# Attention with row maxima: the last step of each unit's maximum made on POOL instead of DVE, with new planner constants

## The chip, the cores and the metric

The kernel runs on one core of one Trainium2 chip. The metric is the device time of one execution in microseconds (us). Five engines work at once, each through its own instruction queue: PE (TensorE, matrix products), ACT (ScalarE, activations), DVE (VectorE, reductions and element-wise work), POOL (GpSimd, element-wise work on SBUF only) and SP, which here issues all transfers. PEld stands for PE's loads of stationary operands.

## The reference, cut to what matters

Two layers share their weights. Each is an attention block and a gated feed-forward block, both behind a layer norm and added to the residual stream. There are 2048 tokens of width 512 in 32 heads of 16, and the hidden width is 1792.

```python
qkv = layernorm(x) @ wqkv                   # q, k, v: 32 heads of 16
scores = einsum("bhqd,bhkd->bhqk", q, k) * 16 ** -0.5
p = softmax(scores, axis=-1)
x = x + reshape(einsum("bhqk,bhkd->bhqd", p, v)) @ wo
h = layernorm(x)
x = x + (gelu(h @ w_gate) * (h @ w_up)) @ w_down
# the same block of two a second time
```

The softmax subtracts each query's maximum over all 2048 keys. The change touches how that maximum is put together.

## The kernel before, in words

**Units.** The work of attention is cut into 72 units. A unit is a group of four heads and a block of queries: 512 queries in seven of the nine query blocks, 256 in the last two of the second layer. Four heads lie in four row groups of PE, 32 partitions each, of which 16 hold the head's coordinates.

**First pass (`p1_emit`, L1579 and L1594).** For 128 queries (`qt`), one head (`j`) and one block of 512 keys (`kb`), PE makes a score tile of 128 x 512 in PSUM, and DVE reduces it, or two tiles at once, to one maximum per query. The maxima go to `PM[:, slot, (qt, kb, j)]`. So a unit of 512 queries gives 4 x 4 x 4 = 64 numbers per partition, a unit of 256 queries 32.

**Folds (`f_emit`, L1398, L1405, L1408; `kd`, L1210; fused step L1589).** For some of these tiles the maximum of two key blocks is taken at once. POOL makes the difference of the two key blocks in `KD`, PE multiplies the queries by it, ACT takes the positive part into a slot of `PT` (a part of `SCR`), and a fused DVE step adds the other block's scores and reduces. The skipped block's entry in `PM` is set to -3e38 by POOL. A fold moves work from DVE to ACT. The planner decides how many there are.

**End of a unit's first pass (`fin`, L950 and L952).** One DVE `tensor_reduce` takes the maximum over the four key blocks, negates it and writes it to `MSEL` in bf16. A DVE transpose puts it into `MT`. Then SP writes it by four small transfers (`negmax`, L971) into an extra row of the queries' operand `QT`. The keys' operand `KT` holds a constant in the same row, +1, which comes from `KBIAS`. So the second pass's product gives score minus maximum with no further step. The three units whose first pass is split (`fin_part`, `fin_rest`, `merge`) and the half unit at the end go other ways with the same signs.

**Second pass (`p2_tile`, `p2_emit`, L1449 and L1425; `pv_emit`, L1473; `nrm`).** PE makes the scores again, with keys as rows, ACT takes the exponential into `PT`, and PE multiplies by the values, with a column of ones that sums the weights, into PSUM bank 7. At a unit's end ACT copies that sum to `ACCS` (L1017), and POOL makes the reciprocals (L1027, a power of -1) and multiplies (L1032).

**The rest.** Projections, the output product and the feed-forward products go through L670, 256-wide where the query block is 256. `evac` and its like (L687, L685) copy their results out of PSUM on ACT or DVE, by how far the first pass is ahead of the second. Some element-wise work follows on POOL: the gate product L1173, the residual sum L1047, parts of the layer norm L719 to L727. In the narrow blocks DVE can do the gate product itself (L1165). L1618 is a filler product of zeros, put where PE would idle.

**The order.** No hardware decides it. `_build` holds a planner, which keeps one clock per engine from stated durations, and in each round takes the next work for PE: a first-pass tile, a second-pass tile, both, a weighted-sum step, a piece of a projection, or a filler. From that come all queues, and `_Sched` puts in the semaphores. Element-wise steps are generators (`_Chain`) that go on when the planner's clocks say that their inputs are ready. Nineteen constants steer the choices. `PLAN` gives a new set for each stretch of 16 first-pass pairs, 129 sets in all. Among them are `SPC`, `SPLIT`, `S1C`, `S2C` (when both passes' tiles are sent together), `LAG` and `LAGT` (how far the first pass may lead), `FL`, `GL`, `FX` (when to fold), and `PIECE`, `GP` (how many matmuls of a projection go in one piece).

Of the kernel before, what the change touches and what calls it, by code (L numbers as in the profile page):

```python
# [6 lines left out]
BF = mybir.dt.bfloat16  # L7
# [303 lines left out]
def _build(nc, x_in, wqkv, wo, wg, wu, wd, out, layer_blocks=((512, 512, 512, 512), (512, 512, 512, 256, 256)),  # L311
# [16 lines left out]
    with es:  # L328
        def sb(name, shape, dt):
            return es.enter_context(nc.sbuf_tensor(name, shape, dt))  # L330
# [1521 lines left out]
```

## Time and profile before

| what | value |
|---|---|
| runs | 2537.78, 2538.1, 2541.32 us (median 2538.1) |
| profiled execution: own time, span | 2542.32 us, 2540.6 us |
| granted clock of PE | 0.998 |
| busy: PE, DVE, ACT, POOL | 2434.9, 2421.7, 2371.5, 591.8 us |
| first-pass reduces on DVE (L1594) | x2489, 2204.7 us |
| exponentials on ACT (L1425) | x2521, 2017.5 us |
| fillers on PE (L1618) | x2408, 425.9 us |
| end-of-unit reduces on DVE (L950) | x69, 17.5 us |
| folds (L1589) | x185 |

The profile is that of one execution, and its own time stands beside the runs' median. Busy time is the time in which an engine had an instruction at work. Matmuls overlap each other, so a PE that is busy is not a PE at its peak. In the rows of groups, the count and busy time come first, then the mean length of one in nanoseconds, then the idle time of the engine just before them with what ended it.

### The profile page before, as it was taken

What the parts mean: (1) busy time and instruction counts of PE and PEld (TensorE: products, weight loads), DVE (VectorE), ACT (ScalarE), POOL (GpSimd) and SP (SyncE); (2) the same over time, 40 slices, a digit from 0 to 9 for tenths busy, and PEclk for the clock granted to TensorE, in tenths of its full rate; (3) what the DMA queues carried; (4) which work ended last, traced back from release to release, by engine and by line L of the source; (5) the groups of instructions that cost most, each with busy time, mean ns of one, the idle gap of its engine ahead of it and who ended that gap; (6) DMA issues with size and microseconds to landing.
All of it is one profiled execution on the core that took longest, in us unless ns stands there. A gap on an engine that the chain in (4) does not pass through costs nothing.

```text
span 2540.6 us, 67774 instructions
## 1 busy us (share of the span) xinstructions
PE 2434.9 (96%) x29660; PEld 1170.1 (46%) x29864; DVE 2421.7 (95%) x3192; ACT 2371.5 (93%) x3270; POOL 591.8 (23%) x743
## 2 busy tenths in 40 slices
PE   8999999999999999999999999999999999999999
PEld 3444443454434444344434455434544445544546
DVE  7999999999999999999998999999999999999993
ACT  7899998999999999999978999999999999989995
POOL 4011122312332213321123211241113211332300
PEclk9999999999999999999999999999999999999999
DMA  3110000000000000000000000000000000000000
GB/s 100 39 56 6 4 9 1 4 2 2 8 1 4 2 3 8 2 4 17 10 6 1 17 2 2 8 3 11 2 8 2 6 6 3 4 3 13 3 8 5
DMA packets 27416, 25.05 MB, mean 10 GB/s; under 512 B 9456, under 2 KB 26096, under 8 KB 27120
## 3 DMA queue, kind: packets, MB, share of 16 engines
q1 hardware_dynamic: 27120, 20.71, 2.8%
q8 instruction: 234, 3.83, 0.6%
q14 instruction: 62, 0.51, 0.1%
HBM read 9.70 MB, written 2.10 MB: 5 GB/s over the span
## 4 chain that ended last, share of the span: by engine, by line
PE 43%; ACT 29%; DVE 26%; issue 1%; POOL 0%; ACTq 0%
ACT SCR L1425 27%; DVE PM L1594 25%; PE PS L1579 13%; PE PS L670 11%; PE PS L1473 9%; PE PS L1449 4%; PE PS L1618 4%; ACT SCR L1405 1%; PE PS L1398 1%; PE PS L768 0%; DVE SCR L1589 0%; ACT AO L1045 0%; ACT XNT L687 0%; ACT ATTT L687 0%; ACT ACCS L1017 0%
## 5 line engine op out<-in xcount | busy, mean ns | idle before, releaser
L1594 DVE TENSOR_REDUCE PM<-PS 128x1 f32<-128x512 f32 (+1 forms) x2489 | 2204.7, 949 | 51.9 <-PE PS L1449 23.3
L1425 ACT ACTIVATE SCR<-PS 128x1024 bf16<-128x1024 f32 (+1 forms) x2521 | 2017.5, 896 | 57.8 <-PE PS L1449 39.5
L1579 PE MATMUL PS<-KT,QT 32*128 32x512 bf16 x3911 | 1006.4, 384 | 36.2 <-DVE PM L1594 19.4
L1449 PE MATMUL PS<-QT,KT 32*128 32x512 bf16 (+1 forms) x4608 | 940.0, 360 | 11.5 <-ACT SCR L1425 8.5
L1473 PE MATMUL PS<-VP,SCR 128*128 128x51 bf16 (+1 forms) x16384 | 806.8, 187 | 12.4 <-ACT SCR L1425 9.5
L1473 PEld LDWEIGHTS PS<-VP,SCR 128*128 128x128 bf16 x16384 | 571.7, 96 | 498.9 <-issue 439.1
L1579 PEld LDWEIGHTS PS<-KT,QT 32*128 32x128 bf16 x3911 | 240.3, 91 | 506.9 <-DVE PM L1594 286.6
L1618 PE MATMUL PS<-WV,ZER 128*128 128x240 bf16 x2408 | 425.9, 267 | 7.7 <-ACT SCR L1425 6.9
L1027 POOL TENSOR_TENSOR RL<-ACCS,CM 128x16 f32<-128x16 f32 (+1 forms) x63 | 173.4, 2753 | 1008.7 <-ACT ACCS L1017 1008.4
L1449 PEld LDWEIGHTS PS<-QT,KT 32*128 32x128 bf16 x4608 | 232.7, 91 | 89.8 <-ACT SCR L1425 60.5
L1618 PEld LDWEIGHTS PS<-WV,ZER 128*128 128x128 bf16 x2408 | 184.6, 97 | 73.7 <-issue 53.0
L1173 POOL TENSOR_TENSOR HT<-HT,AO 128x512 bf16<-128x512 bf16 (+1 forms) x112 | 123.1, 1101 | 261.9 <-ACT AO L1171 261.8
L1210 POOL TENSOR_TENSOR KD<-KT 128x512 bf16<-128x512 bf16 x71 | 81.8, 1154 | 207.3 <-PE PS L1398 188.2
L1405 ACT ACTIVATE SCR<-PS 128x512 bf16<-128x512 f32 (+1 forms) x132 | 103.7, 786 | 23.5 <-PE PS L1398 23.2
L1589 DVE CUSTOM_DVE_ANT_0 SCR<-PS,SCR 128x512 bf16<-128x512 f32 x185 | 119.6, 686 | 4.0 <-PE PS L1579 2.7
L670 PE MATMUL PS<-XNT,WU 128*128 128x512 bf16 (+1 forms) x444 | 116.4, 354 | 6.6 <-issue 5.5
L670 PE MATMUL PS<-WD,HT 128*128 128x512 bf16 x378 | 114.3, 380 | 8.0 <-issue 6.5
L670 PE MATMUL PS<-XNT,WG 128*128 128x512 bf16 (+1 forms) x488 | 117.1, 357 | 2.1 <-issue 1.0
L1047 POOL TENSOR_TENSOR X<-X,AO 128x512 f32<-128x512 f32 x45 | 57.1, 1268 | 212.1 <-ACT AO L1045 212.0
L1152 ACT ACTIVATE HT<-PS 128x512 bf16<-128x512 f32 (+1 forms) x126 | 69.1, 550 | 31.8 <-PE PS L670 29.3
L1171 ACT ACTIVATE AO<-PS 128x512 f32<-128x512 f32 (+1 forms) x112 | 65.6, 586 | 2.0 <-PE PS L670 1.3
L670 PEld LDWEIGHTS PS<-XNT,WG 128*128 128x128 bf16 x504 | 39.6, 97 | 54.8 <-issue 31.1
(106 smaller groups left out, 883.2 us busy)
## 6 DMA issues: line engine op xcount, KB each, us to landing
KT<-SG SPq DMA_DIRECT2D x64, 64.0 KB
QT<-MT SPq DMA_DIRECT2D x236, 1.0 KB
QT<-SG SPq DMA_DIRECT2D x56, 64.0 KB
out_dram<-AO SPq DMA_DIRECT2D x16, 128.0 KB, 1.7
WG<-in_B_w_gate_dram SPq DMA_DIRECT2D x4, 448.0 KB, 5.0
WU<-in_B_w_up_dram SPq DMA_DIRECT2D x4, 448.0 KB, 4.8
WD<-in_B_w_down_dram SPq DMA_DIRECT2D x4, 384.0 KB, 4.9
QT<-MT SPq DMA_DIRECT2D x68, 0.5 KB
```

The lines of the kernel that those rows point to most:

```text
L670: ins = e.matmul(out_ap, lhsT=l, rhs=r_, start=(i == 0), stop=(i == n - 1))
L1027: emit("pool", lambda e: e.tensor_tensor(RL[:, s, 0:4 * nq], lsum, CM1[:, 0:4 * nq], op=ALU.pow), r=[("ACCS", s), ("CM1",)], w=[("RL", s)] ...
L1173: emit("pool", lambda e, ft=ft, o=o: e.tensor_tensor(HT[:, ft, 0:n], HT[:, ft, 0:n], AO[:, o, 0:n], op=ALU.mult), r=[("AO", o), ("HT", ft) ...
L1210: emit("pool", lambda e: e.tensor_tensor(KD[:, s, :], KT[:, g, ka * 512:(ka + 1) * 512], KT[:, g, kb * 512:(kb + 1) * 512], op=ALU.subtrac ...
L1405: emit("act", lambda e: e.activation(PT[:, s0:s0 + cnt, :], PS[:, bk:bk + cnt, :], ACTF.Relu), r=bks, w=[("PT", s0 + d) for d in range(cnt ...
L1425: emit("act", lambda e: e.activation(dst, src, ACTF.Exp, scale=DH ** -0.5), r=[BK[bk + i] for i in range(cnt)], w=[("PT", i) for i in slot ...
L1449: ins = e.matmul(bank(bk)[:, i * n:(i + 1) * n], lhsT=KT[32 * j:32 * j + 32, g, kt * 128:(kt + 1) * 128], rhs=QT[32 * j:32 * j + 32, s, 0: ...
L1473: ins = e.matmul(acc, lhsT=PT[:, slot, i * n + qt * 128:i * n + (qt + 1) * 128], rhs=AP(VP, (kt * H + 4 * g + j) * 17, [[NTT * H * 17, 128 ...
L1579: ins = e.matmul(bank(b), lhsT=QT[32 * j:32 * j + 32, s, qt * 128:(qt + 1) * 128], rhs=KT[32 * j:32 * j + 32, g, kb * 512:(kb + 1) * 512], ...
L1589: emit("dve", lambda e, i=i, b=b, sl=sl: e.tensor_tensor_reduce(PT[:, sl, :], bank(b), PT[:, sl, :], 1.0, -3.0e38, ALU.add, ALU.max, po[:, ...
L1594: emit("dve", lambda e: e.tensor_reduce(po, PS[:, bs[0]:bs[0] + cnt, :], axis=AX.X, op=ALU.max), r=bks, w=[("PM", sm) + h[1:] for h in hs] ...
L1618: return e.matmul(PS[:, b, NACC:512], lhsT=ZER[:, :], rhs=WV[:, 0, 0:512 - NACC], start=(b != 7), stop=(b != 7), skip_group_check=True)
```

## The change

The end-of-unit maximum of 65 of the 72 units is made by POOL. `fin` hands those units to the new `fin_pool`, which makes the maximum of two numbers as x - y, its positive part, plus y. It does that for key blocks 0 with 1 and 2 with 3 in one go, then for the two results: six POOL instructions. The transpose stays on DVE and now waits for POOL. The last four units and the three split ones stay on the DVE reduce. The maximum is no longer negated, so the constant in the keys' extra row becomes -1, and `fin_part`, `fin_rest` and `merge` change their signs to match.

`PLAN` gets two more columns, `PB` and `OVF`. `PB` over 1 holds a weighted-sum step back until `PB` of them are ready while PE is in row groups (33 sets). `OVF` lets projection work run over while PE works as one array (49 sets are not 0). The other columns change in 126 of 129 sets. New code for a layer norm on POOL (`ln_pool`) is switched off (`LNP=0`), and `NSG=3` keeps the number of staging buffers. A few of the sets and all of the rest:

```diff
 PLAN = [
-    (0.0, 0.25, 0.45, 0.42, 0.3, -0.05, 1, 1, 70, 84, 8, 60, 0.3, 2.0, 0, 2, 2, 2, 7),
-    (0.1, 0.2, 0.65, 0.62, 0.3, -0.05, 1, 1, 62, 84, 8, 60, 0.3, 2.0, 0, 2, 2, 2, 7),
...
+    (0.1, 0.1, 0.45, 0.42, 0.3, -0.05, 1, 1, 62, 84, 8, 60, 0.3, 2.0, 0, 2, 2, 1, 7, 1, 0.0),
+    (0.1, 0.1, 0.45, 0.42, 0.3, -0.05, 2, 1, 62, 84, 8, 60, 0.1, 2.0, 0, 2, 2, 2, 7, 1, -0.1),
...
-            emit("pool", ... e.affine_select(KBIAS[:, 0:1], KBIAS[:, 0:1], [[0, 1]], ALU.not_equal, 1.0,
+            emit("pool", ... e.affine_select(KBIAS[:, 0:1], KBIAS[:, 0:1], [[0, 1]], ALU.not_equal, -1.0,
...
 def fin_part(u):
-            emit("dve", lambda e: e.tensor_reduce(mo, pin, axis=AX.X, op=ALU.max, negate=True),
+            emit("dve", lambda e: e.tensor_reduce(mo, pin, axis=AX.X, op=ALU.max),
...
 def fin_rest(u):
-            emit("dve", lambda e: e.tensor_scalar(do, pin, -1.0, 0.0, op0=ALU.mult, op1=ALU.min),
+            emit("dve", lambda e: e.tensor_scalar(do, pin, 0.0, None, op0=ALU.max),
...
+        def fin_pool(u):
+            s1 = u % n_ahead
+            nq = units[u][3] // 128
+            pv = PM[:, s1, 0:nq * 4 * NKB].rearrange("p (a k j) -> p a k j", a=nq, j=4)
+            mo = MSEL[:, s1, 0:4 * nq].rearrange("p (j a) -> p a j", j=4)
+            kk = [("PM", s1, qt, kb, j) for qt in range(nq) for kb in range(4) for j in range(4)]
+            yield ("pool", kk, [])
+            for w, x, y, o, ok, d in ((2, pv[:, :, 0::2, :], pv[:, :, 1::2, :], pv[:, :, 1::2, :], kk, 0.055 * nq / 4),
+                                      (1, pv[:, :, 1, :], pv[:, :, 3, :], mo, [("MSEL", s1)], 0.03 * nq / 4)):
+                emit("pool", lambda e, x=x, y=y: e.tensor_tensor(x, x, y, op=ALU.subtract), r=kk, w=kk, dur=0.19 + d)
+                emit("pool", lambda e, x=x: e.tensor_scalar(x, x, 0.0, None, op0=ALU.max), r=kk, w=kk, dur=0.19 + d / 2)
+                emit("pool", lambda e, x=x, y=y, o=o: e.tensor_tensor(o, x, y, op=ALU.add), r=kk, w=ok, dur=0.19 + d)
+            yield ("dve", [("MSEL", s1)], [("MT", s1)])
+            emit("dve", lambda e: e.transpose(MT[:, s1, :], MSEL[:, s1, :]),
+                 r=[("MSEL", s1)], w=[("MT", s1)], dur=0.13)
+            fin_rec.add(u)
+            add(negmax(u), -1e6 + u)
...
 def fin(u):
-            emit("dve", lambda e: e.tensor_reduce(mo, pin, axis=AX.X, op=ALU.max, negate=True),
+            if FNP and u < NU - 4 and u not in split and NKB == 4:
+                return add(fin_pool(u), -1e6 + u)
+            emit("dve", lambda e: e.tensor_reduce(mo, pin, axis=AX.X, op=ALU.max),
...
+            if PB > 1 and mode[0] == "row" and G is not None and G < now + 0.4 and work and work[-1][0] == 1:
+                n_rdy = 0
+                for q in pvq[:PB]:
+                    if est([("PT", q[1])]) <= now + 0.03:
+                        n_rdy += 1
+                if n_rdy < PB and pt_busy.count(None) > 1:
+                    work.pop()
             for pr, t, cost, fn, due, at in work:
                 over = (SO if seam else OV if can_p2[0] else URG) if due < pos["p1"] - DUEM and pr > 1 else 0.0
+                if mode[0] == "full" and pr > 1:
+                    over += OVF
```

More of the change, by code (lines that the diff above doesn't have):

```diff
@@ L311, in _build @@
 def _build(nc, x_in, wqkv, wo, wg, wu, wd, out, layer_blocks=((512, 512, 512, 512), (512, 512, 512, 256, 256)),
-           n_ahead=6, n_pre=6, S1C=0.45, S2C=0.42, OV=0.3, PD=80, FDUE=20, LIM=-0.05, NT=1, AHD=2.0, DUEM=2, FDL2=0, OPD=12, URG=0.3, ft_tok=512, n_pt=8, n_qt=8, SPLIT=0.15, SPC=0.1, PVC=47, WARM=0.55, WARML=0.42, NPV=7, BOOST=0.0, LAG=62, LAGT=84, GP=2, SING=0, DUE=0, END=360, LAGE=10, FD=205, FDL=-10, QD=32, KD_=16, VD=20, FL=8, FMAX=6, NKD=2, FLOOK=2, FX=0.3, GF=1, NSPL=3, HSPL=0, TSPL=1, HNA=3, TNA=3, HV=16, TW=0.95, HF=60, VS=14, SO=1.0, SF=1, SP=0, FAST=1, TG=0, GS=2, P2B=1, PIECE=2, GL=60, GLE=20, HARD=-1e9):
+           n_ahead=6, n_pre=6, S1C=0.45, S2C=0.42, OV=0.3, PD=80, FDUE=20, LIM=-0.05, NT=1, AHD=2.0, DUEM=2, FDL2=0, OPD=12, URG=0.3, ft_tok=512, n_pt=8, n_qt=8, SPLIT=0.15, SPC=0.1, PVC=47, WARM=0.55, WARML=0.42, NPV=7, BOOST=0.0, LAG=62, LAGT=84, GP=2, SING=0, DUE=0, END=360, LAGE=10, FD=205, FDL=-10, QD=32, KD_=16, VD=20, FL=8, FMAX=6, NKD=2, FLOOK=2, FX=0.3, GF=1, NSPL=3, HSPL=0, TSPL=1, HNA=3, TNA=3, PB=1, OVF=0.0, LNP=0, FNP=1, NSG=3, LNT=12, HV=16, TW=0.95, HF=60, VS=14, SO=1.0, SF=1, SP=0, FAST=1, TG=0, GS=2, P2B=1, PIECE=2, GL=60, GLE=20, HARD=-1e9):
     S = x_in.shape[1]
@@ L350, in _build @@
         QT = sb("QT", [128, n_qt, 512], BF)
-        SG = sb("SG", [128, 3, 512], BF)
+        SG = sb("SG", [128, NSG, 512], BF)
         HT = sb("HT", [128, NFT, ft_tok], BF)
@@ L368, in _build @@
         DW = sb("DW", [128, NSB, 16], F32)
+        LS = sb("LS", [128, 512], F32) if LNP else None
         KD = sb("KD", [128, NKD, 512], BF)
@@ L535, in _build @@
         for j in range(4):
-            emit("pool", lambda e, j=j: e.affine_select(KBIAS[:, 0:1], KBIAS[:, 0:1], [[0, 1]], ALU.not_equal, 1.0,
+            emit("pool", lambda e, j=j: e.affine_select(KBIAS[:, 0:1], KBIAS[:, 0:1], [[0, 1]], ALU.not_equal, -1.0,
                                                         base=-(32 * j + 1), channel_multiplier=1),
@@ L708, in ln_fast, with ln_sum @@
                 at["xn"] = i
+        def ln_sum(i, xa, xk, first, col, dur):
+            yield ("pool", [xk] + ([] if col == 0 else [("LNS", i)]), [("LS",)])
+            first()
+            w = D // 4
+            while w >= 16:
+                yield ("pool", [], [])
+                emit("pool", lambda e, w=w: e.tensor_tensor(LS[:, 0:w], LS[:, 0:w], LS[:, w:2 * w], op=ALU.add),
+                     r=[("LS",)], w=[("LS",)], dur=0.18 + w / 520.0)
+                w //= 2
+            yield ("dve", [("LS",)], [("MV", i)])
+            emit("dve", lambda e, i=i: e.tensor_reduce(MV[:, i, col:col + 1], LS[:, 0:16], axis=AX.X, op=ALU.add),
+                 r=[("LS",)], w=[("MV", i)], dur=0.09)
@@ new lines, in ln_pool, with first, second @@
+        def ln_pool(tts, x_of, ready, at):
+            for i, tt in enumerate(tts):
+                xa, xk = x_of(tt)
+                yield ("cond", lambda tt=tt: ready(tt))
+                def first():
+                    emit("pool", lambda e: e.tensor_tensor(LS[:, 0:D // 2], xa[:, 0:D // 2], xa[:, D // 2:D], op=ALU.add),
+                         r=[xk], w=[("LS",)], dur=0.18 + D / 1040.0)
+                def second():
+                    emit("pool", lambda e: e.tensor_scalar(LS[:, 0:D], xa, 1.0, LNS[:, 2, i:i + 1], op0=ALU.mult, op1=ALU.add),
+                         r=[xk, ("LNS", i)], w=[("LS",)], dur=0.77)
+                    emit("pool", lambda e: e.tensor_tensor(LS[:, 0:D], LS[:, 0:D], LS[:, 0:D], op=ALU.mult),
+                         r=[("LS",)], w=[("LS",)], dur=0.18 + D / 520.0)
+                    emit("pool", lambda e: e.tensor_tensor(LS[:, 0:D // 2], LS[:, 0:D // 2], LS[:, D // 2:D], op=ALU.add),
+                         r=[("LS",)], w=[("LS",)], dur=0.18 + D / 1040.0)
+                yield from ln_sum(i, xa, xk, first, 0, 0)
+                yield ("pool", [("MV", i)], [("LNS", i)])
+                emit("pool", lambda e, i=i: e.tensor_scalar(LNS[:, 2, i:i + 1], MV[:, i, 0:1], -1.0 / D, None, op0=ALU.mult),
+                     r=[("MV", i)], w=[("LNS", i)], dur=0.24)
+                yield from ln_sum(i, xa, xk, second, 1, 0)
+                yield ("pool", [("MV", i)], [("LNS", i)])
+                emit("pool", lambda e, i=i: e.tensor_scalar(LNS[:, 0, i:i + 1], MV[:, i, 1:2], 1.0 / D, LN_EPS, op0=ALU.mult, op1=ALU.add),
+                     r=[("MV", i), ("LNS", i)], w=[("LNS", i)], dur=0.24)
+                emit("pool", lambda e, i=i: e.tensor_tensor(LNS[:, 1, i:i + 1], LNS[:, 0, i:i + 1], CM05[:, i:i + 1], op=ALU.pow),
+                     r=[("LNS", i), ("CM05",)], w=[("LNS", i)], dur=0.59)
+                yield ("cond", lambda i=i: at["tr"] > i - 2)
+                yield ("pool", [xk, ("LNS", i)], [("XN", i % 2)])
+                emit("pool", lambda e, i=i, xa=xa: e.tensor_scalar(
+                    XN[:, i % 2, :], xa, LNS[:, 2, i:i + 1], LNS[:, 1, i:i + 1], op0=ALU.add, op1=ALU.mult),
+                    r=[xk, ("LNS", i)], w=[("XN", i % 2)], dur=0.77)
+                at["xn"] = i
@@ L784, in ln_to_xnt @@
             else:
-                add((ln_fast if fast else ln_head)(tts, x_of, ready, at), due)
+                by_pool = LNP and tag != ("in", 0) and not fast and (tag == ("mid", NL - 1) or tts[0] < LNT)
+                add((ln_fast if fast else ln_pool if by_pool else ln_head)(tts, x_of, ready, at), due)
             for i, tt in enumerate(tts):
@@ L795, in ln_to_xnt @@
             locks["XN"] = False
-        sg_free = [0, 1, 2]
+        sg_free = list(range(NSG))
         def proj(W, wkey, c, cols, n, tts):
@@ L917, in merge @@
             yield ("pool", [("MSEL", s1), ("MSB", i)], [("DW", i)])
-            emit("pool", lambda e: e.tensor_tensor(DW[:, i, 0:4 * nq], sgn[0], sgn[1], op=ALU.subtract),
+            emit("pool", lambda e: e.tensor_tensor(DW[:, i, 0:4 * nq], sgn[1], sgn[0], op=ALU.subtract),
                  r=[("MSB", i), ("MSEL", s1)], w=[("DW", i)], dur=0.2)
@@ L1634, in _build @@
                 if stretch[0] < len(PLAN):
-                    SPC, SPLIT, S1C, S2C, OV, LIM, NT, P2B, LAG, LAGT, FL, GL, FX, AHD, DUE, DUEM, PIECE, GP, NPV = PLAN[stretch[0]]
+                    SPC, SPLIT, S1C, S2C, OV, LIM, NT, P2B, LAG, LAGT, FL, GL, FX, AHD, DUE, DUEM, PIECE, GP, NPV, PB, OVF = PLAN[stretch[0]]
                 stretch[0] += 1
```

254 rows, old and new, of the table PLAN are left out of this document.

## The prediction

> **What bounds the kernel now.** I read the head of the page and its chain that ended last (shares by engine), then the busy times by stretch (columns: PE, PEld, DVE, ACT, POOL).
>
> ```profile
> span 2540.6 us, 67774 instructions
> PE 2434.9 (96%) x29660; PEld 1170.1 (46%) x29864; DVE 2421.7 (95%) x3192; ACT 2371.5 (93%) x3270; POOL 591.8 (23%) x743
> ...
> PE 43%; ACT 29%; DVE 26%; issue 1%; POOL 0%; ACTq 0%
> ...
> 100.00:1200.00 1100.00, 1057.26 (x13058) 503.35 (x13143) 1081.74 (x1457) 1058.84 (x1376) 259.11 (x331) 1.00 0.03 9
> 1200.00:1500.00 300.00, 288.60 (x3240) 131.09 (x3265) 281.94 (x361) 271.25 (x384) 76.25 (x94) 1.00 0.03 7
> 1500.00:2440.00 940.00, 908.25 (x11562) 440.46 (x11642) 920.11 (x1168) 896.42 (x1288) 224.87 (x248) 1.00 0.02 5
> 2440.00:2540.60 100.60, 95.25 (x1218) 58.48 (x1216) 57.16 (x91) 72.54 (x103) 3.32 (x8) 0.95 0.02 6
> ```
>
> Between 100 and 2440 us DVE idles 18.3 + 18.1 + 19.9 = 56 us, ACT 41 + 29 + 44 = 114 us. So DVE is the tighter of two nearly full engines: what leaves DVE shortens the span as long as ACT can follow, and ACT has some 58 us more room. PE's 96% is softer: it holds 2408 filler matmuls (L1618), issued only where nothing else was ready. POOL is three quarters idle. The chain passes between the three full engines in thousands of short pieces, so none of them is the bound alone. Next, the groups with the shapes kept apart.
>
> ```profile
> L1594 DVE TENSOR_REDUCE PM<-PS 128x2 f32<-128x1024 f32 x1237 | 1491.9, 1219 | 37.9 <-PE PS L1449 17.3 <-PE PS L1579 9.0 <-PE PS L1398 0.2
> L1594 DVE TENSOR_REDUCE PM<-PS 128x1 f32<-128x512 f32 x1252 | 844.3, 683 | 13.9 <-PE PS L1449 6.0 <-PE PS L1579 2.0 <-PE PS L1398 0.7
> L952 DVE STREAM_TRANSPOSE MT<-MSEL 128x32 bf16<-128x32 bf16 x69 | 14.6, 212 | 2.4
> L950 DVE TENSOR_REDUCE MSEL<-PM 128x16 bf16<-128x64 f32 x53 | 14.2, 268 | 1.8
> ```
>
> The score reduces are nearly all of DVE. The step that the change moves is the last row: once per unit, it reduces the four key blocks' maxima to one. Its place, in the timeline of DVE (start, length):
>
> ```profile
> 74.16 1.22 DVE L1594 TENSOR_REDUCE PM<-PS 128x2 f32<-128x1024 f32 x1
> 75.41 0.27 DVE L950 TENSOR_REDUCE MSEL<-PM 128x16 bf16<-128x64 f32 x1
> 75.71 0.21 DVE L952 STREAM_TRANSPOSE MT<-MSEL 128x32 bf16<-128x32 bf16 x1
> 75.85 0.65 DVE L1589 CUSTOM_DVE_ANT_0 SCR<-PS,SCR 128x512 bf16<-128x512 f32 x1
> 76.42 0.08 DVE L1589 DVE_READ_ACCUMULATOR2_ANT PM<- 128x1 f32 x1
> ```
>
> **The sum.** Counts are from the instruction orders of the two built kernels, durations from this execution (span 2540.6, own time 2542.3; the median shown is 2538.1, 4.2 lower).
>
> *Reduce removed from DVE.* 65 of the 69 go (53 wide, 12 narrow; the last four units and the three split ones keep theirs). From its start to the transpose's is 75.71 - 75.41 = 0.30 us. The narrow form means (17.5 - 14.2) / 16 = 0.206 us, say 0.24 with its gap. 53 x 0.30 + 12 x 0.24 = 18.8 us off DVE, 16.7 by busy time alone. The 65 transposes stay.
>
> *Fewer folds.* A fold lets ACT take the positive part of a difference of two blocks, so that DVE skips one of them and runs a fused step on the other. The new constants make 173 instead of 185. Plain heads: 3726 cost 2204.7 us merged, 0.592 each; 24 more are +14.2 us. Fused steps follow each other at 0.61 us (76.42 to 77.03 and on; the first of that row at 0.57), 12 fewer are -7.3. DVE: +6.9 us. ACT loses 12 x 103.7 / 185 = 6.7 us.
>
> *Exponentials and evacuations.* 12 double exponentials become 24 single: at 1.068 and 0.610 us that is +1.8 us on ACT. Five 256-wide gate products return from ACT with POOL (0.449 us each, -2.2) to DVE (0.425, +2.1); two 0.69-us evacuations leave DVE and a 256-wide one (0.4) comes: -1.0; ACT gets +0.8. DVE in all: -18.8 + 6.9 + 2.1 - 1.0 = -10.8 us; ACT: -6.7 + 1.8 - 2.2 + 0.8 = -6.3 us. Both fall, so ACT does not become the limit in DVE's place.
>
> *PE's switches.* PE works in row groups (L1579, L1449, L1398) or as one array (the others). The order changes between the two 5518 times before, 5342 after: 176 fewer, where the constants PB (hold a weighted-sum step until several are ready) and OVF (let projections run over) act. Price:
>
> ```profile
> 700.82 0.39 PE L670 MATMUL PS<-XNT,WG 128*128 128x512 bf16 x1
> 701.14 0.39 PE L1579 MATMUL PS<-KT,QT 32*128 32x512 bf16 x2
> 701.46 0.82 PE L670 MATMUL PS<-XNT,WG 128*128 128x512 bf16 x3
> ```
>
> Three array matmuls in a row take 0.82, so they follow at (0.82 - 0.39) / 2 = 0.215 us; after a single one the row group starts 0.32 later. A switch costs 0.105 us, 176 of them 18.5 us of PE. Where PE idles or fills it buys nothing (0). PE has 43% of the chain that ended last: 8 us at most. I take 4, since DVE's waits for L1449 and L1579 come to only 34 us.
>
> *Tail.* After the last score matmul 40 exponential tiles of 512 remain instead of 38: +1 us of ACT with DVE idle.
>
> *POOL's chain and the new wait.* Each unit gets six POOL steps: subtract, positive part and add over 32 elements, then over 16. The nearest rows: tensor-tensor on 16 elements (L918) 0.220 us, on 272 (L926) 0.658, so 1.7 ns per element; tensor-scalar on 1 element (L723) 0.243, on 512 (L727) 0.774, so 1.0 ns. That makes 0.247 + 0.275 + 0.247 + 0.22 + 0.26 + 0.22 = 1.47 us. Dependent POOL steps start 0.08 to 0.10 after each other's end:
>
> ```profile
> 7.55 0.24 POOL L719 TENSOR_SCALAR LNS<-MV 128x1 f32<-128x1 f32 x1 [2.38 <-DVE MV L717]
> 7.87 0.57 POOL L721 TENSOR_TENSOR LNS<-LNS,CM 128x1 f32<-128x1 f32 x1
> 8.53 0.25 POOL L723 TENSOR_SCALAR LNS<-MV 128x1 f32<-128x1 f32 x1
> ```
>
> Five such gaps make 1.9 us. The upper bound is the strided 128x256 row (L1032), 0.621 us a step: 4.2 us. I take 1.9, the small rows being the near ones. POOL's busy time rises by about 65 x 1.47 = 95 us, to 27%. The transpose now waits on DVE for that chain, and the next score reduces queue behind it, and PE's score banks behind them. In the new order 2.4 to 7.7 us of other DVE work stand between a unit's last reduce and its transpose (62 units counted, median 3.8), so a chain of 1.9 us costs 0. The query maxima reach PE some 4 us later; score heads lead exponential tiles by 58 or more from head 200 to 3700 (46 before), about 34 us of reduces, so that hides too. KBIAS's sign and the other sign changes cost nothing: same instructions.
>
> The Trainium skill (GPSIMD Engine Reference, Engine selection) speaks against the change: elementwise work on VectorE, about 2x slower on GpSimd. By that rule, with the chain on the path, each unit would pay 1.9 for 0.3 us, +104 us in all; the trace, with POOL idle for 77% of the span, speaks for cover instead.
>
> Sum: -10.8 - 4 + 1 = -13.8 us. The profiled execution would take 2528.5, the median 2524.3 us.
>
> **Rivals.**
>
> *DVE stalls at the transpose (slower).* POOL's work stands in one queue. Ahead of the chain are 23 times a key difference (1.15 us), 12 times a gate product that waits for an ACT copy, 11 times the normalisation of 0.4 to 0.6 us behind a power of 1.6 to 2.9 us that waits for ACT. For: POOL's waits for ACT are its longest (1008 us before L1027). Against: the order gives most units over 3.4 us. Against the counted covers a chain of 3.5 us stalls 18 units by 11 us in sum; with 13.8 us gained the break-even is about 3.6 us. At 4.2 us, 42 units lose 34 us: 2538 - 14 + 34 = 2558. Smaller excesses end between 2533 and 2543.
>
> *The gain is swallowed (same).* Nearly every constant row is changed (126 of 129), and none of that idle time can be priced from here. If DVE's 56 us of mid-span idle grow by a quarter, 14 us, the time stays at 2538. For: ACT is at 96%, so a bad mix of the two in one stretch costs at once. Against: both engines have less to do.
>
> *The constants gain more (faster still).* If the same 56 us fall by a quarter, and the switches bring their full 8 us: 2524 - 14 - 4 = 2506.
>
> That the reduce stays on DVE is excluded: only 7 of these are left in the new DVE order.
>
> SBUF contention is the other way a busier POOL could hurt DVE. The Trainium skill (GPSIMD Engine Reference, Specifications) has it only for DVE work in a two-port mode or with two SBUF inputs. The reduces on L1594 read PSUM, and I give it no chance of its own.
>
> **The numbers.** Forecast, between 2513 and 2533: 0.60. More gain: 0.16. Swallowed, 2533 to 2543: 0.13. Stalls or a worse mix, over 2543: 0.11. A measurement tells about 0.2% (5 us) here. So faster 0.76, same 0.13, slower 0.11. The range goes from the bigger gain's end, 2507, to 2541, where the swallowed case is mostly inside; some 2 in 10 stay outside.
>
> **What would show it.** Right: DVE busy near 2411 and ACT near 2365, POOL near 690; POOL steps at 0.2 to 0.28 us; the transposes with no idle before them named after POOL; some 5340 switches and a chain with less PE. Wrong: idle before the transpose released by POOL, of tenths of a us in dozens of units (first rival), or L1594's idle above 52 us, waiting for L1449 and L1579 (second).

## The result and the profile after

| kernel | median (us) | range (us) |
|---|---|---|
| before, runs beside after | 2539.71 | 2537.78 to 2541.44 (4) |
| before, in the three later sessions | 2537.61, 2537.94, 2537.31 | 2535.4 to 2541.4 (19, 19, 12) |
| after | 2524.30 | 2523.95 to 2524.91 (4) |

After takes 0.994 of before (95% interval 0.9923 to 0.9957). The forecast was 2524.3. Two of the four runs of before beside after took 2541 us, as did later runs with a clock of 0.998, while the rest had 1.0. Against the medians of the later sessions the gain is 13.0 to 13.6 us, and that is the figure used below. The profiled execution of before had 12.4 us of half clock near its end, so the two spans differ by 18.4 us, some 5 more than the medians.

The page of after: head, busy times, shares of the chain that ended last, then the busy times by stretch (PE, PEld, DVE, ACT, POOL).

```profile
span 2522.2 us, 68091 instructions
PE 2409.2 (96%) x29682; PEld 1161.1 (46%) x29881; DVE 2403.7 (95%) x3131; ACT 2353.2 (93%) x3267; POOL 683.9 (27%) x1119
PE 42%; DVE 32%; ACT 24%; issue 1%; POOL 0%; ACTq 0%
100.00:1200.00 1100.00, 1052.67 (x13179) 503.76 (x13267) 1084.27 (x1433) 1059.25 (x1383) 307.26 (x508) 1.00 0.03 9
1200.00:1500.00 300.00, 288.17 (x3225) 131.06 (x3250) 284.19 (x361) 265.41 (x368) 80.29 (x118) 1.00 0.03 8
1500.00:2440.00 940.00, 905.62 (x11690) 439.95 (x11768) 912.29 (x1152) 898.43 (x1313) 262.73 (x420) 1.00 0.02 6
```

DVE has 18.0 us less to do than before (2421.7), ACT 18.3 less, POOL 92 more. DVE's idle time between 100 and 2440 us is 15.7 + 15.8 + 27.7 = 59.2 us, against 56. So these 2340 us hold about as much idle time as before, and DVE's work simply ends earlier. DVE's share of the chain rose from 26 to 32%, ACT's fell from 29 to 24.

DVE's groups with the shapes kept apart: the reduces of 65 units are gone, and nothing is named as idle time before the 65 transposes (last figure of the last row).

```profile
L1663 DVE TENSOR_REDUCE PM<-PS 128x2 f32<-128x1024 f32 x1237 | 1492.2, 1216 | 39.6 <-PE PS L1518 19.3 <-PE PS L1648 9.3 <-PE PS L1467 0.4
L1663 DVE TENSOR_REDUCE PM<-PS 128x1 f32<-128x512 f32 x1276 | 856.8, 680 | 12.4 <-PE PS L1518 4.8 <-PE PS L1648 1.1
L1000 DVE STREAM_TRANSPOSE MT<-MSEL 128x32 bf16<-128x32 bf16 x65 | 13.0, 200 | 0.0
```

One unit's chain and the step ahead of it in POOL's timeline (start, length), with the first step's wait from the list of waits behind it:

```profile
724.55 1.16 POOL L1242 TENSOR_TENSOR HT<-HT,AO 128x512 bf16<-128x512 bf16 x1
725.67 0.25 POOL L996 TENSOR_TENSOR PM<-PM 128x32 f32<-128x32 f32 x1
726.01 0.29 POOL L997 TENSOR_SCALAR PM<-PM 128x32 f32<-128x32 f32 x1
726.38 0.25 POOL L998 TENSOR_TENSOR PM<-PM 128x32 f32<-128x32 f32 x1
726.71 0.22 POOL L996 TENSOR_TENSOR PM<-PM 128x16 f32<-128x16 f32 x1
727.02 0.24 POOL L997 TENSOR_SCALAR PM<-PM 128x16 f32<-128x16 f32 x1
727.35 0.23 POOL L998 TENSOR_TENSOR MSEL<-PM 128x16 bf16<-128x16 f32 x1
...
POOL PM L996 <- DVE PM L1663: 373.9, 41, 28.9
```

The chain takes 727.58 - 725.67 = 1.91 us. Its first step waits for DVE's last reduce 41 times. In most of the other 24 units POOL was still at earlier work when that reduce ended, as here, where the gate product of L1242 runs right up to the chain.

### The profile page after: what moved, and what is told of

Its sections match the earlier page's. It is cut to its first block, busy times and chain, and to the rows that moved or that the text cites. A ratio compares the mean times of both kernels' runs of the same rounds, so it can differ in the third digit from the quotient of the medians.

```text
span 2522.2 us, 68091 instructions
## 1 busy us (share of the span) xinstructions
PE 2409.2 (96%) x29682; PEld 1161.1 (46%) x29881; DVE 2403.7 (95%) x3131; ACT 2353.2 (93%) x3267; POOL 683.9 (27%) x1119
## 4 chain that ended last, share of the span: by engine, by line
PE 42%; DVE 32%; ACT 24%; issue 1%; POOL 0%; ACTq 0%
DVE PM L1663 30%; ACT SCR L1494 22%; PE PS L1648 14%; PE PS L671 12%; PE PS L1542 9%; PE PS L1687 4%; PE PS L1518 3%; ACT SCR L1474 1%; DVE SCR L1658 1%; PE PS L816 1%; ACT AO L1114 0%; PE PS L1467 0%; ACT XNT L688 0%; ACT ATTT L688 0%; ACT SG L688 0%
## 5 line engine op out<-in xcount | busy, mean ns | idle before, releaser
L1663 DVE TENSOR_REDUCE PM<-PS 128x1 f32<-128x512 f32 (+1 forms) x2513 | 2216.6, 944 | 52.0 <-PE PS L1518 24.1
L1494 ACT ACTIVATE SCR<-PS 128x1024 bf16<-128x1024 f32 (+1 forms) x2533 | 2008.2, 899 | 59.2 <-PE PS L1518 43.4
L1518 PE MATMUL PS<-QT,KT 32*128 32x512 bf16 (+1 forms) x4608 | 924.0, 360 | 7.5 <-ACT SCR L1494 6.3
L1242 POOL TENSOR_TENSOR HT<-HT,AO 128x512 bf16<-128x512 bf16 (+1 forms) x107 | 119.5, 1119 | 236.9 <-ACT AO L1240 236.9
L996 POOL TENSOR_TENSOR PM<-PM 128x16 f32<-128x16 f32 (+2 forms) x130 | 30.2, 232 | 379.1 <-DVE PM L1663 373.9
L1658 DVE CUSTOM_DVE_ANT_0 SCR<-PS,SCR 128x512 bf16<-128x512 f32 x173 | 111.7, 685 | 3.1 <-PE PS L1467 0.6
L1474 ACT ACTIVATE SCR<-PS 128x512 bf16<-128x512 f32 (+1 forms) x121 | 97.1, 802 | 18.7 <-PE PS L1467 18.3
```

Source lines behind the costliest of these rows:

```text
L1242: emit("pool", lambda e, ft=ft, o=o: e.tensor_tensor(HT[:, ft, 0:n], HT[:, ft, 0:n], AO[:, o, 0:n], op=ALU.mult), r=[("AO", o), ("HT", ft) ...
L1474: emit("act", lambda e: e.activation(PT[:, s0:s0 + cnt, :], PS[:, bk:bk + cnt, :], ACTF.Relu), r=bks, w=[("PT", s0 + d) for d in range(cnt ...
L1494: emit("act", lambda e: e.activation(dst, src, ACTF.Exp, scale=DH ** -0.5), r=[BK[bk + i] for i in range(cnt)], w=[("PT", i) for i in slot ...
L1518: ins = e.matmul(bank(bk)[:, i * n:(i + 1) * n], lhsT=KT[32 * j:32 * j + 32, g, kt * 128:(kt + 1) * 128], rhs=QT[32 * j:32 * j + 32, s, 0: ...
L1658: emit("dve", lambda e, i=i, b=b, sl=sl: e.tensor_tensor_reduce(PT[:, sl, :], bank(b), PT[:, sl, :], 1.0, -3.0e38, ALU.add, ALU.max, po[:, ...
L1663: emit("dve", lambda e: e.tensor_reduce(po, PS[:, bs[0]:bs[0] + cnt, :], axis=AX.X, op=ALU.max), r=bks, w=[("PM", sm) + h[1:] for h in hs] ...
```

## The experiments

Two theories stood at the start. **The prediction's:** DVE is the tighter engine in either order, so what leaves it shortens the time by its length, and the new constants matter through the counts of work. **The rival:** the three full engines hold each other, so what DVE time is worth depends on the order of all the work around it. Removing the step and re-ordering the work have to be tried apart.

### The order of after with the reduce on DVE (`reduce_back`)

```diff
-    (six POOL steps of fin_pool)
+    sch.op("dve", lambda e: e.tensor_reduce(mo, pin, axis=AX.X, op=ALU.max), r=kk, w=[("MSEL", s1)])
     (transpose, unchanged)
```

> The changed kernel with its order on every other engine kept, but the 65 maxima made by a DVE reduce right ahead of the transpose and POOL's six steps left out. If the DVE time that the move frees is worth its full length (my theory), 53 x 0.30 + 12 x 0.24 = 18.8 us come back: 2540 to 2545 us. If the gain came from the new constants and the order they make (rival), DVE has slack for the reduce and the time stays within 5 us of 2524.

Measured: 2531.79 us (2529.87 to 2533.93, 10 runs), 0.9979 of before (0.9969 to 0.9988), which lies between the two expectations. So in the new order the removal is worth 7.5 us, and the new order alone, with the reduce still on DVE, 5.8 us. The reduce does occupy DVE for what the prediction said. DVE's timeline of this kernel, then of after, at the end of the same unit:

```profile
728.45 4.72 DVE L1670 TENSOR_REDUCE PM<-PS 128x2 f32<-128x1024 f32 x5
733.09 0.26 DVE L1006 TENSOR_REDUCE MSEL<-PM 128x16 bf16<-128x64 f32 x1
733.38 0.21 DVE L1007 STREAM_TRANSPOSE MT<-MSEL 128x32 bf16<-128x32 bf16 x1
```

```profile
724.15 4.72 DVE L1663 TENSOR_REDUCE PM<-PS 128x2 f32<-128x1024 f32 x5
728.79 0.20 DVE L1000 STREAM_TRANSPOSE MT<-MSEL 128x32 bf16<-128x32 bf16 x1
```

With the reduce the transpose starts 4.93 us after the five score reduces began, without it 4.64 us: 0.29 us, as priced. Yet of some 19 us in all only 7.5 arrive. The chain of `reduce_back` says how far DVE is the limit there:

```profile
DVE 41%; PE 37%; ACT 21%; issue 1%; POOL 0%; ACTq 0%
```

### No maximum at all, in each order (`no_maximum_before`, `no_maximum_after`)

```diff
-    emit("dve", lambda e: e.tensor_reduce(mo, pin, ...), ...)      # before's order
+    plan_only("dve", ...)      # planned as before, not issued; last four units as they were
```

In the order of after the six POOL steps are planned and not issued.

> The kernel before, its order kept, with the DVE reduce of 65 units left out (part of the computation is missing: the transpose takes zeros). It prices the reduce in the old order with no help from POOL or from constants. My theory: DVE is the limit in most places, so 15 to 19 us of the 18.8 go, 2520 to 2525. Rival (gain from the constants): under 5 us, 2534 or more.

> The changed kernel with its order kept and the maximum of these 65 units left out on all engines (no POOL steps, the transpose takes a tile of zeros; part of the computation is missing). If POOL's chain is fully covered (my theory), nothing changes: 2522 to 2526 us. If the chain still costs something, by DVE waiting for it, by queueing POOL's other work or by SBUF traffic (rival), it is faster by more than 3 us, under 2521.

Measured: in before's order 2536.82 us (2535.97 to 2543.10, 10 runs), 0.9998 of before (0.9989 to 1.0007). In after's order 2524.83 us (2524.62 to 2525.28), no faster than after itself. The second is plain: to within 0.5 us the POOL chain and the new wait cost nothing. The first is the main finding: in the old order the reduce was worth 0.8 us, although DVE does 16 us less. Its score reduces by shape, its stretches and its chain:

```profile
L1602 DVE TENSOR_REDUCE PM<-PS 128x2 f32<-128x1024 f32 x1237 | 1491.4, 1217 | 49.5 <-PE PS L1457 26.0 <-PE PS L1587 11.7 <-PE PS L1406 0.6
L1602 DVE TENSOR_REDUCE PM<-PS 128x1 f32<-128x512 f32 x1252 | 842.7, 681 | 17.8 <-PE PS L1457 8.7 <-PE PS L1587 2.7 <-PE PS L1406 0.7
...
100.00:1200.00 1100.00, 1070.32 (x13151) 503.64 (x13149) 1074.51 (x1427) 1058.64 (x1376) 259.26 (x331) 1.00 0.03 9
1200.00:1500.00 300.00, 291.29 (x3272) 131.28 (x3270) 281.00 (x357) 271.43 (x385) 76.22 (x94) 1.00 0.03 7
1500.00:2440.00 940.00, 917.06 (x11649) 440.69 (x11645) 913.69 (x1139) 896.45 (x1289) 224.97 (x248) 1.00 0.02 5
...
PE 45%; ACT 29%; DVE 25%; issue 1%; POOL 0%; ACTq 0%
```

The idle time before the score reduces is 49.5 + 17.8 = 67.3 us, against 37.9 + 13.9 = 51.8 before: 15.5 us more, for 16.0 us of work removed. DVE idles 25.5 + 19.0 + 26.3 = 70.8 us between 100 and 2440 us, against 56. The freed time became waiting for PE, above all for the second pass's score tiles (L1457, which is L1449 of before: 26.0 + 8.7 us against 17.3 + 6.0). ACT's busy times in the same stretches are those of before to within 0.2 us.

The four medians of the two orders side by side:

| | reduce on DVE | reduce gone from DVE | worth |
|---|---|---|---|
| order of before | 2537.6 | 2536.8 | 0.8 |
| order of after | 2531.8 | 2524.8 (2524.3 with POOL's steps) | 7.0 to 7.5 |

### Do the fillers swallow the freed time? (`fewer_fillers_before`, `fewer_fillers_at_maxima`, `fewer_fillers_after`)

PE's queue holds its fillers in fixed places. If they stand where DVE would now be early, they keep the tiles late.

```diff
+    n_wm[0] += 1
-    emit_pe(warm_fn(b), ...)
+    emit_pe(warm_fn(b), ..., skip=n_wm[0] % 12 == 0)      # every 12th filler planned, not issued
```

In `fewer_fillers_at_maxima`, which also leaves out the 65 reduces, the three fillers behind each of them go instead.

> The kernel before with every twelfth filler left out (198 of 2408, 21 us of PE) and nothing else. It is the control for the run above. Theory: with the reduce in place DVE is as late as PE, so most of it is swallowed: 2532 to 2537. If fillers as such hold up everything: 2525 or less. If they fill waits alone: 2536 to 2539; if PE's clock falls for want of them: above 2540.

> The kernel before with the 65 maxima left out, as in the run where this alone gained nothing, and in addition the next three fillers on PE behind each of them left out (195 of 2408; each about 0.107 us of PE). Theory now: PE's queue is fixed when the kernel is built, fillers included, so time freed on DVE turns into waiting for PE; with 0.3 us of fillers gone at the same place it is paid out: 10 us or more, 2520 to 2528. Rival: ACT paces those places, or the fillers lie in waits, and nothing changes: 2534 to 2538.

> The changed kernel with every twelfth filler left out (200 of 2425, 21 us of PE) and nothing else. Theory: its order already uses the freed DVE time, so PE is not ahead of the others as a pacer: 2520 to 2525. If PE's queue with its fillers paces it: 2515 or less, a version faster than both. If the clock falls: above 2527.

Measured: 2534.11 us without 198 fillers in before (10 runs), 3.8 less than before's 2537.94 beside it. 2540.57 for `fewer_fillers_at_maxima` (2533.59 to 2548.64, 10 runs); only the run at full clock reaches 2533.6, 3 us under `no_maximum_before`, and the others had a mean clock of 0.993 to 0.999. Without the fillers behind the maxima the kernel thus gains no more than it does without as many fillers anywhere. So the fillers explain 3 of the 15 us at most, and the theory mostly falls. What else keeps PE's tiles from coming earlier in the old order stays open. `fewer_fillers_after` takes 2521.84 us (2521.41 to 2521.99), 0.9935 of before (0.992 to 0.995). It is below every run of after, though those were made on another occasion. It is the fastest kernel of this study.

### The constants with and without POOL's steps (`pool_old_constants`, `new_constants_no_pool`, `no_pb_ovf`)

Here the planner makes its order anew.

```diff
-PLAN = [(0.1, 0.1, ..., 7, 1, 0.0), ...]     # after
+PLAN = [(0.0, 0.25, ..., 7, 1, 0.0), ...]    # pool_old_constants: before's 19 columns, PB = 1, OVF = 0
-FNP=1
+FNP=0                                        # new_constants_no_pool: all units on the DVE reduce
-(..., 1, -0.1) ...
+(..., 1, 0.0) ...                            # no_pb_ovf: the two last columns without effect
```

> The kernel after, POOL's steps included, but with the 19 old constants per stretch, and PB and OVF without effect; the planner then makes a new order: 5558 switches of PE, 155 folds, 2507 fillers. Priced by the rows of the profiles and its own counts, DVE has 2426.8 us of work, against 2419.4 before and 2408.6 after. The prediction's theory (what leaves DVE leaves the time, in any order; the constants only through counts): 2524 + 18 = 2542 us. Rival A (the POOL steps are the gain, the constants are not needed for it): 2524 to 2530. Rival B (an order that no constants were chosen for leaves both engines idle besides): over 2546.

> The kernel after with all its constants, but every unit's maximum by the DVE reduce again, and the order planned anew for that: 5396 switches, 184 folds, 2543 fillers; DVE's counted work is 2423.4 us, 14.8 above that of after. The prediction's theory: 2524 + 15 = 2539 us. Rival A (the constants carry the gain by themselves, also without POOL): 2524 to 2532, at or below the 2531.8 that the reduce had in the order of after. Rival B (constants and POOL steps belong together, any other order of the same planner is worse): over 2543.

> The kernel after with PB and OVF without effect in every stretch, all else as it is, planned anew: 5504 switches against 5342, 152 folds against 173, DVE's counted work 2424.0 us against 2408.6. By the prediction's price of DVE time 2524 + 15 = 2539 us, and with the switches at 4 us in 176 another 4: 2543. If the switches cost their full 0.105 us (162 of them, 17 us) on top of DVE: 2556. If neither counts: 2524 to 2530.

Measured (median, ratio to before with its 95% interval):

| | reduce on DVE | steps on POOL |
|---|---|---|
| old constants | 2537.3 (before) | 2576.8 (1.0159, 1.0144 to 1.0174) |
| new constants | 2566.6 (1.0112, 1.0097 to 1.0127) | 2524.3 (after) |
| new constants, no PB and OVF | | 2553.2 (1.0059, 1.0043 to 1.0076) |

Rival B holds for the first two, and `no_pb_ovf` comes near the dearest of its three cases. Either half of the change alone, planned anew, makes the kernel slower by 29 to 40 us, and only both together make it faster. The pages show two sources, here for `pool_old_constants` and `new_constants_no_pool`: busy times, and the last unit's maximum in DVE's timeline.

```profile
PE 2461.7 (96%) x29755; PEld 1179.4 (46%) x29963; DVE 2424.5 (94%) x3135; ACT 2359.1 (92%) x3276; POOL 673.5 (26%) x1106
...
2512.11 0.21 DVE L1019 TENSOR_REDUCE MSEL<-PM 128x8 bf16<-128x32 f32 x1
```

```profile
PE 2448.6 (95%) x29800; PEld 1180.5 (46%) x29999; DVE 2430.6 (95%) x3220; ACT 2369.4 (92%) x3304; POOL 587.6 (23%) x735
...
2505.59 0.21 DVE L1019 TENSOR_REDUCE MSEL<-PM 128x8 bf16<-128x32 f32 x1
```

In after that last maximum stands at 2470.2, so these two end their first pass 42 and 35 us later, with 21 and 27 us more busy time on DVE and the rest idle. Their tails behind it (spans 2575.3 and 2564.8) are 63 and 59 us, against 52. The constants decide how many blocks are folded and how far each pass leads, and in these runs each set served only the kernel that it was made for. No set was sought for either half alone, so the table doesn't say what either could reach with constants of its own. Which of the 21 columns does it is open too: apart from PB and OVF together they weren't tried one by one.

### How long may the chain be? (`chain_medium`, `chain_longer`, `chain_uncovered`)

```diff
     emit("pool", lambda e, x=x: e.tensor_scalar(x, x, 0.0, None, op0=ALU.max), ...)
+    for _ in range(6 if w == 2 else 0):      # 4 in chain_medium
+        sch.op("pool", lambda e, x=x: e.tensor_scalar(x, x, 0.0, None, op0=ALU.max), r=kk, w=kk)
```

`chain_uncovered` puts the six POOL steps into before's order, with the transpose right behind the last reduce.

> The order of after, with four more positive parts (which change nothing in the result) between the first three and the last three POOL steps, so the chain takes 1.9 + 4 x 0.36 = 3.35 us. By the covers that the prediction counted, a chain of that length stalls DVE by 9 us in all: 2533 us. By the run with six more steps (4.2 us, stall of 60 us in 61 of 65 units, clock at 0.97, +118 us) the covers are some 0.9 us each shorter than counted: a stall of some 20 to 25 us at the transpose, and if the clock falls again, 2550 to 2580; if stalls of this length leave the clock alone, 2545 to 2550.

> The changed kernel with POOL's positive part over 32 elements done six more times for each of the 65 units (it changes no value; 0.29 us and a gap of 0.08 each), all orders kept: the chain takes 4.2 us in place of 1.9. By the counted covers 42 of 62 units then stall DVE, 34 us in sum (my prediction's price): 2550 to 2562. If DVE time is worth about 0.4 of its length in this order, as the run with the reduce put back gave (7.4 of 18.8): 2535 to 2542. If PE's clock falls as in the uncovered run: above 2565.

> The kernel before, its order kept, with the maximum of 65 units made by the six POOL steps but the DVE transpose left where it was, right behind the last score reduce. My theory: each unit pays 1.9 us of chain on DVE's path in place of 0.30, and more where POOL is in the middle of something: +104 us or more, some 2640 (2610 to 2680). Rival: PE and the score banks absorb the wait, and it costs under 20 us.

Measured: 2548.83 us (2542.99 to 2555.94, 9 runs) with a chain of 3.4 us, 2642.55 (2639.20 to 2647.66) with 4.1 us, 2778.41 (2769.30 to 2805.32) uncovered, which is far above the 2610 to 2680 expected. In the same sequence, the transpose's line in DVE's list of waits (us in all, times, longest):

```profile
DVE MT L1002 <- POOL MSEL L1000: 19.7, 31, 1.1
```

```profile
DVE MT L1002 <- POOL MSEL L1000: 60.3, 61, 1.9
```

```profile
DVE MT L966 <- POOL MSEL L965: 148.0, 65, 5.6
```

The covers that the prediction counted gave 18 units and 11 us for a chain of 3.5 us, 42 units and 34 us for 4.2. The runs show about twice that, so the covers are some (60.3 - 34) / 61 = 0.4 us thinner than counted. The trace of after agrees: in the 48 units in which it names what released the chain, DVE reaches the transpose 2.3 to 4.1 us behind that release, median 3.4, where the count gave 2.4 to 7.7 and 3.8. In other units POOL starts late besides. For the chain of 1.91 us it makes no difference: every transpose of after starts at least 0.28 us behind its chain's end.

The other part of the price is the clock. PEclk over the span for `chain_longer`, one of its stretches (mean clock third from the end), and PEclk for `chain_uncovered`:

```profile
PEclk9998899999999999999999999999999999999999
...
200.00:400.00 200.00, 186.27 (x2234) 88.49 (x2238) 176.66 (x240) 175.28 (x204) 41.14 (x90) 0.87 0.02 6
```

```profile
PEclk9689879999999988898699989899998899899999
```

The trace's clock record has 2, 22 and 45 spells of half clock in these three profiled executions, 20, 156 and 478 us in all. Stalls of 60 us cost 118 us against after, and stalls of 148 us cost 241 against before. Time at half clock can add half its length at most, 78 and 239 us, so it has room for the difference, but the two parts were not taken apart. `chain_medium` shows the stalls nearly alone: four of its nine runs had a clock of 1.0 and took 2543.0 to 2543.3 us, 19 more than after, about the length of the 19.7 us of stalls in its profiled run. The 18.8 us of short reduces put back into the same order cost 7.5. Why stalls of 0.6 us cost their length and reduces of 0.3 us less than half is not shown.

## Why the prediction was right, and where its steps were not

The total was right by the cancelling of two errors, so that hitting it to a tenth was luck. By its own terms the prediction said -18.8 us for the removal and +5 for everything else (8.0 of DVE work, -4 for the switches, +1 for the tail). Measured: -7.5 for the removal in the new order, -5.8 for the new order.

**Reduce removed from DVE, -18.8 us: the length was right, the worth was not.** 65 reduces left and each had held DVE for 0.29 us. The step that failed is the sentence that what leaves DVE shortens the span as long as ACT can follow. In before's order it brought 0.8 us and in after's 7.5. The profile of before had the warning in it: DVE carried 26% of the chain that ended last, and 26% of 18.8 is 4.9 us. In `reduce_back` it carried 41%, and 41% of 18.8 is 7.7 us. The share is no law (0.8 was less than 4.9, and the stalls of `chain_medium` cost their full length), but for the reduce it was the nearer measure, and the prediction used it for PE's switches while it gave DVE its full length.

**Folds, exponentials, evacuations: right in size on DVE, not on ACT.** The score reduces grew by 2216.6 - 2204.7 = 11.9 us (14.2 predicted). The fused steps fell by 9.1 us with their readouts (7.3). The 256-wide gate products grew by 2.0 us (2.1). DVE's busy time went to 2403.7 instead of 2411. ACT's fell by 18.3 us to 2353.2, instead of by 6.3 to 2365. The folds' positive parts gave what was predicted (103.7 to 97.1). But the exponentials, said to grow by 1.8 us, fell from 2017.5 to 2008.2:

```profile
L1494 ACT ACTIVATE SCR<-PS 128x1024 bf16<-128x1024 f32 (+1 forms) x2533 | 2008.2, 899 | 59.2 <-PE PS L1518 43.4
```

The mean lengths of both forms rose a little (1068 to 1074 ns, 610 to 617), so they overlap each other more; the prediction counted them one by one. ACT's total is 2355.7 in `reduce_back` too, so this belongs to the order.

**PE's switches, credited with 4 us: probably too small.** The second pass's score matmuls, the same 3584 in both orders, before and after:

```profile
L1449 PE MATMUL PS<-QT,KT 32*128 32x512 bf16 x3584 | 814.3, 384 | 10.0 <-ACT SCR L1425 7.5 <-DVE AO L1191 0.2 <-ACT SCR L1405 0.2
```

```profile
L1518 PE MATMUL PS<-QT,KT 32*128 32x512 bf16 x3584 | 800.8, 384 | 6.7 <-ACT SCR L1494 5.8 <-DVE AO L1260 0.2
```

They occupy PE for 13.5 us less with the same mean length, so they stand closer together. The row is 801.7 us in `reduce_back`, so it belongs to the order and not to POOL. The rows of groups overlap one another, so their changes don't add up to PE's. The traces of before and after also lack some 200 matmul records each, so PE's totals are best compared in the two kernels without a maximum, old order first:

```profile
PE 2454.4 (97%) x29864; PEld 1168.0 (46%) x29864; DVE 2405.7 (95%) x3127; ACT 2370.1 (94%) x3270; POOL 592.1 (23%) x743
```

```profile
PE 2433.6 (96%) x29881; PEld 1161.3 (46%) x29881; DVE 2403.8 (95%) x3131; ACT 2353.4 (93%) x3267; POOL 590.5 (23%) x729
```

PE is busy 20.8 us less in the new order, near the 18.5 us of 176 switches at 0.105. How much of it arrives cannot be read off singly. But PE's time and ACT's are the large savings of the new order that the rows show, and the order gained 5.8 us with DVE's added work in it.

**The constants** were weighed as a mishap or as a bonus of idle time. In fact they are half of the change: with the old ones the kernel with POOL's steps is 39.5 us slower than before. The prediction had no row for that, and its other half, the new DVE order, could be counted only because the built kernel was at hand.

**Tail, +1 us:** from the last unit's maximum to the end 51.8 us, against 50.1 in `no_maximum_before`, which has before's order at full clock: +1.7.

**POOL's chain:** 1.91 us against 1.9 predicted, +92 us busy against 95, no idle time at the transpose, and leaving the steps out gains nothing. By the rule of the Trainium skill (GPSIMD Engine Reference, Engine selection) this work belongs on VectorE. The trace agrees that POOL takes longer, 1.91 us against 0.29. But as long as the result isn't needed at once, on an engine that is 77% idle, that costs nothing: 2524.3 with the six steps, 2524.8 without any maximum. With the chain on the path it does: +241 us in `chain_uncovered`, more than twice the +104 that the prediction worked out, because each wait was 148.0 / 65 = 2.3 us instead of 1.9 and the clock fell too.

**Rivals.** DVE stalling at the transpose did not happen, but its price was too low: a chain of 4.1 us costs 118 us, not 34. The swallowed gain did happen, in before's order, where the prediction didn't look for it: the new order is what released it. A quarter less idle time did not come: 59 us against 56.

## What to carry to other kernels

Where several engines are nearly full, what leaves the busiest of them can be worth much less than its length (0.8 and 7.5 of 18.8 us here). As a first guess, ask what share of the chain that ended last that engine carries, in the order in which the work will really run, and look for the freed time as a wait for the next engine. A step can go to a slower, idle engine for nothing if enough independent work stands between its input and its user; measure that cover with room to spare, since a stall that repeats costs PE's clock as well. Constants of a planner can fit one sequence of events only, so a changed step and its constants are judged together.

## What the runs showed of the hardware

The clock fell with stalls that look harmless one by one. With waits of 1 us on average (60.3 us in 61 units, longest 1.9) there were 22 spells of half clock in 2.6 ms, with a mean length of 156 / 22 = 7 us. With stalls of 0.6 us on average (19.7 us in 31) there were 2. PE's own longest wait behind them, in its list of waits of `chain_longer`:

```profile
PE PS L1650 <- DVE PM L1665: 89.7, 206, 1.9
```

The clock record and PE's matmuls (their ends are modelled), laid side by side, show when a spell begins. All spells of `chain_longer` but the last, which the end of the program cuts off, last one to seven times 3.413 us and begin on one grid of that step. Twenty of them begin between 40 and 2480 us. In the step just before each of these PE idled for 1.0 to 2.2 us in sum; in the 651 other steps there at full clock it idled for 1.12 us at most. One beginning, by steps (PE's busy time first, the clock third from the end):

```profile
142.11:145.53 3.42, 3.10 (x40) 1.56 (x41) 3.28 (x5) 3.42 (x4) 1.46 (x6) 1.00 0.00 0
145.53:148.94 3.41, 1.97 (x33) 1.03 (x32) 1.85 (x5) 2.06 (x3) 1.76 (x8) 1.00 0.00 0
148.94:152.35 3.41, 3.41 (x28) 1.73 (x25) 3.23 (x4) 2.68 (x3) 0.00 (x0) 0.51 0.27 66
```

So in that run about 1 us of idle PE within one step was the limit, and a single gap of 1.4 us, as here, was enough. It is not the whole rule: one spell of `reduce_back` followed a step with 0.46 us of idle time, and the spell of 10.2 us near the end of before one with none.

The Trainium skill (TensorE: Matmul & The Clock Gate, HAM oscillation) puts the danger at idle gaps of PE of over about 3.4 us. Here 1.9 us was the longest wait for DVE and the clock fell all the same. The Trainium skill has a second failure mode (TensorE: Matmul & The Clock Gate, A second HAM failure mode: psum-queue depth-cycling), short idle times between groups of matmuls that come often enough. That is nearer to this trace, though here one such gap in a step could do it.

Fillers seem to work against this, but not each one earns its place: without every twelfth the two kernels gained 2.5 and 3.8 us, while without the three behind each maximum the clock of `fewer_fillers_at_maxima` was below 1.0 in nine of ten runs, down to 0.993, against one of ten in `no_maximum_before`.
